# The last 2 KB a partition of wq moved from the sync queue to a GpSimd DMA whose source has eight outer rows

## The chip, the cores and the metric

The kernel runs on one core of one Trainium2 chip. The metric is device time in microseconds (us) of one execution; less is better. The profiled execution lists its engines as PE (TensorE matmul) and PEld (its weight load), DVE (VectorE), ACT (ScalarE), POOL (GpSimd) and SP (SyncE). Sixteen DMA engines move data between HBM and SBUF for this core.

## The reference

One decode step for two batch rows (B = 2, D = 512): a layer norm of x, a sliding-window attention over a cache, and a gated MLP that multiplies it.

```python
x = A_x                                  # (2, 1, 512)
xn = layernorm(x)
# attention: 32 query heads of 128, 8 kv heads, the last W = 4096 keys of 32768
q = (xn @ wq).reshape(B, 1, 32, 128)     # wq: 512 x 4096
s = softmax(q k^T * 128**-0.5) v         # k, v: (2, 8, 4096, 128) of the cache, each kv head for 4 query heads
s = s.reshape(B, 1, 4096) @ wo           # wo: 4096 x 512
# MLP: w_in 512 x 1792, Fh = 896, w_out 896 x 512
z = gelu(xn @ w_in); z1, z2 = z[:896], layernorm(z[896:])
g = silu((z1 * (z2 * w_sp + b_sp)) @ w_out)
return x + s * g
```

Everything is float32. The inputs that are read add up to the 89.4 MB that the DMA table of the profile lists: the k and v windows are 16 loads of 4 MB, wq 8 MB, wo 8 MB, w_in 3.5 MB, w_out 1.75 MB.

## The kernel before

**Loads.** Big loads go out on the sync (SP) queue in a fixed order: win, wout, wq, then k0, k1, v0, k2, v1, ... k7, v6, v7, then wo. They live in a ring of four slots of 32 KB a partition (`ring`, `bufs=4`): a load is issued when the tile that held its slot before has been read for the last time. `slot()` makes such a tile. wout uses the `kts` pool. The loop at lines 127 to 131 makes the two wq tiles: the one for k = 0, 1 is loaded by one DMA, the one for k = 2, 3 by two DMAs of 16 KB a partition each (2 MB each). With `wq_v = wq.rearrange("(p k) f -> p k f")`, partition p of plane k holds row 4p + k of wq. Four small loads (x, w_sp, b_sp and x again as x4) go out on the scalar (ACT) queue. GpSimd (POOL) issues no DMA; it clears constant tiles with memsets at the start (`nc.gpsimd.memset`) and builds the identity.

**Layer norm and transposed x.** On DVE `bn_stats`, `bn_aggr` and a few small steps give `xn` (2 x 512). Four PE transposes bring it into `pt` with partition p of plane k holding feature 4p + k, and a DVE copy puts it into `xnT` (128 x 4 x 32, the 30 other columns zero).

**First matmuls.** PE multiplies xnT with win (32 matmuls, `z`), turns z (28 matmuls, `zT_ps`), then the query projection: `queries(k)` issues eight matmuls for plane k, over r = 0, 1 and g = 0 to 3, with the 512 columns `c = (r * G + g) * 512` of `wqt[k]`, summed over k in two PSUM banks. `queries(3)` is the last. Then come y (hT with wout), two ACT copies `qs`, two DVE transposes `qx`, two DVE multiplies `xm`, one matmul `qa`, and `place_queries` (DVE, tile `qb`).

**Attention.** Eight units of two kv heads each run through steps whose order is written out by hand in `ORDER`: eight DVE transposes of the k tile into `kts`, score matmuls `sh`, softmax, DVE transposes `pT`, matmuls `acc` with v. Then wo: `part` for the blocks that can be multiplied early, and `so` for the last unit's rows. The second wo tile is loaded in pieces of 16, 8, 4, 2 and 2 KB a partition, and the last eight `so` matmuls take the last piece. The end is two DVE operations `res` and one store.

InOrder keeps PE, DVE, ACT and SP instructions in program order. POOL's order is left to the scheduler.

Of the kernel before, what the change touches and what calls it, by code (L numbers as in the profile page):

```python
# [9 lines left out]
F32 = mybir.dt.float32  # L10
# [4 lines left out]
P = 128  # L15
HQ, DH = 32, 128
# [4 lines left out]
def free_ap(t, offset, dims):  # L21

    return bass.AP(tensor=t.tensor, offset=t.offset + offset, ap=[list(t.ap[0])] + [list(d) for d in dims])
# [47 lines left out]
def kernel(  # L71
# [13 lines left out]
    nc = tc.nc  # L85
    pe, dve, act, sp = (InOrder(tc, e) for e in (nc.tensor, nc.vector, nc.scalar, nc.sync))
    B, _, D = x.shape
# [7 lines left out]
    KT = D // P  # L95
# [3 lines left out]
    DC = D // G  # L99
    SCALE = DH ** -0.5  # L100
    OFF = 30000.0 / SCALE

    fit = ctx.enter_context(tc.tile_pool(name="fit", bufs=1))
    fit.tile([P, 480], F32, tag="fit", name="fit")
# [2 lines left out]
    cst = ctx.enter_context(tc.tile_pool(name="cst", bufs=1))  # L107
# [3 lines left out]
    def slot(name, *shape):  # L111
        return ring.tile([P, *shape], F32, tag="slot", name=name)

    def bank(name, *shape):
        return ps.tile([P, *shape], F32, tag="kt", name=name, bufs=2)
# [9 lines left out]
    wq_v = wq.rearrange("(p k) f -> p k f", p=P)  # L125
    wqt = []
    for a in range(0, KT, 2):
        t = slot(f"wq{a}", 2, HQ * DH)
        for k, n in ((0, 2),) if a == 0 else ((0, 1), (1, 1)):
            sp.dma_start(t[:, k : k + n], wq_v[:, a + k : a + k + n, :])  # L130
        wqt += [t[:, 0], t[:, 1]]

    wb1 = cst.tile([1, 2], F32, tag="wb1", name="wb1")
# [21 lines left out]
    ident = cst.tile([P, P], F32, tag="ident", name="ident")  # L155
    make_identity(nc, ident)
    selw = cst.tile([P, 60], F32, tag="selw", name="selw")
    nc.gpsimd.memset(selw, 0.0)
    xnT = cst.tile([P, KT, 32], F32, tag="xnT", name="xnT")
    nc.gpsimd.memset(xnT, 0.0)  # L160
    ones = cst.tile([P, P], F32, tag="ones", name="ones")
    nc.gpsimd.memset(ones, 1.0)
# [29 lines left out]
    rsqrt(rs, va, "x")  # L192
    xn = sb.tile([B, D], F32, tag="o", name="xn", bufs=1)
    dve.tensor_scalar(xn, xs, mv[:, 0:1], rs, op0=ALU.subtract, op1=ALU.mult)
    pt = bank("xnT_ps", KT, B)
    for k in range(KT):
        pe.transpose(pt[:, k, :], xn.rearrange("b (p k) -> b k p", k=KT)[:, k, :], ident[:B, :B])
    dve.tensor_copy(xnT[:, :, :B], pt)

    same = cst.tile([P, G, 32], F32, tag="same", name="same")  # L200
# [15 lines left out]
    dve.tensor_reduce(other, free_ap(rowm, 0, [[4, 2], [8, REP]]), axis=AX.X, op=ALU.add)  # L216
    dve.tensor_scalar(other, other, -OFF, OFF, op0=ALU.mult, op1=ALU.add)
    diag = cst.tile([P, 4], F32, tag="diag", name="diag")
# [33 lines left out]
    pt = bank("zT_ps", 2, FT, B)  # L252
# [7 lines left out]
    pq = [ps.tile([P, 512], F32, tag=f"s{r}", name=f"q_ps{r}") for r in range(NR)]  # L260

    def queries(k):
        for r in range(NR):
            for g in range(G):
                c = (r * G + g) * 512
                pe.matmul(
                    pq[r][32 * g : 32 * g + 32, :], xnT[:, k, :], wqt[k][:, c : c + 512],
                    start=(k == 0), stop=(k == KT - 1),
                )

    queries(0)
    zT = cst.tile([P, 2, FT, B], F32, tag="zT", name="zT")
    dve.tensor_copy(zT, pt)
# [19 lines left out]
    per_b = [[0, FT], [1, B]]  # L293
    mean_over_rows(mean, z2, "mean_ps")
    queries(1)
    dve.tensor_scalar_mul(mean, mean, 1.0 / FH)
    dve.tensor_sub(z2, z2, free_ap(mean, 0, per_b))
# [5 lines left out]
    dve.tensor_scalar(z2, z2, wb[:, 0:1], wb[:, 1:2], op0=ALU.mult, op1=ALU.add)  # L303
    dve.tensor_mul(hT[:, :, 0 : 16 * B : 16], z1, z2)
    queries(2)
    queries(3)

# [286 lines left out]
    for u in range(NU):  # L594
        p = Unit()
        p.u, p.m, p.kt, p.sh, p.ss, p.s, p.p, p.pT = u, None, {}, {}, {}, {}, {}, {}
        units.append(p)
    for line in ORDER.strip().split("\n"):
        for name in line.split():
            name, at = name.split(":")  # L600
            u, _, a = at.partition(".")
# [34 lines left out]
```

## Time and profile before

| what | value |
|---|---|
| median of 3 runs | 216.96 us (216.91 to 217.72) |
| the profiled execution's own time | 217.3 us |
| its span, first to last instruction | 215.4 us |
| mean granted TensorE clock | 0.834 |
| busy: PE, DVE, ACT, POOL | 139.0, 125.7, 51.1, 5.2 us |
| HBM bytes read | 89.40 MB |

The span is 1.9 us shorter than the execution's own time, and that execution is 0.34 us above the median. In the profile, a group of instructions is listed as line, engine, operation, output tile <- input tiles, then counts and times; "L65" is the helper that issues every instruction of the in-order engines. A DMA group is listed where it is issued; "DMA k<-in_A_k_cache_dram" in the chain of work means that the time was spent until such a load had landed. The windows view gives, for each stretch, the busy time of each engine, the granted clock, the mean busy share of the 16 DMA engines, and GB/s.

### The profile page before, as it was taken

To read this page: it belongs to the slowest core of one execution; us is meant where nothing else is said; L and a number is where in the kernel's file an instruction comes from. 1 tells how busy PE (TensorE), PEld (TensorE's weight loads), DVE (VectorE), ACT (ScalarE), POOL (GpSimd) and SP (SyncE) were. 2 spreads that over 40 slices of the span, in tenths; PEclk is the share of its full clock that TensorE was granted. 3 is DMA by queue.
4 is the path that set the end of the run, shared out by engine and by line. 5 is a ranking of instruction groups with operands and counts; after the bars stand their busy time and mean duration, and the time that the engine had idled before them with its cause. 6 is when DMAs were issued, how large, how long until landed. Compare 5 with 4: busy or idle time off the path is not lost.

```text
span 215.4 us, 2476 instructions
## 1 busy us (share of the span) xinstructions
PE 139.0 (65%) x972; PEld 50.7 (24%) x972; DVE 125.7 (58%) x217; ACT 51.1 (24%) x128; POOL 5.2 (2%) x19
## 2 busy tenths in 40 slices
PE   0179594503857985934890796289359628988893
PEld 0118431300111222302230231113113211243242
DVE  2511212349799899639927981994698099535001
ACT  5010203200116036122330503151251306152210
POOL 8000000000000000000000000000000000000000
PEclk9999589955785799995899599559859985997999
DMA  7999999999999999999999999999999999999990
GB/s 256 427 438 456 396 435 456 408 458 408 463 414 441 426 426 444 417 458 408 450 420 444 423 420 450 426 450 417 438 415 444 432 420 456 405 463 402 414 377 29
DMA packets 3930, 89.54 MB, mean 416 GB/s; under 512 B 446, under 2 KB 462, under 8 KB 848
## 3 DMA queue, kind: packets, MB, share of 16 engines
q1 hardware_dynamic: 3900, 89.40, 96.8%
q8 instruction: 7, 0.11, 0.2%
q14 instruction: 3, 0.02, 0.0%
q10 hardware_dynamic: 20, 0.01, 0.0%
HBM read 89.40 MB, written 0.00 MB: 415 GB/s over the span
## 4 chain that ended last, share of the span: by engine, by line
DMA 68%; DVE 23%; ACT 3%; PE 2%; issue 1%; SPq 1%
DMA k<-in_A_k_cache_dram 51%; DVE kts L65 18%; DMA wo<-in_A_wo_dram 12%; DMA win<-in_B_w_in_dram 5%; DVE pT L65 2%; ACT p L65 2%; PE sh L65 2%; DVE m L65 1%; DVE gate L65 1%; SPq L65 1%; DVE nb L65 1%; PE s L65 1%; DVE qb L65 1%; ACT ss L65 0%; DVE res L65 0%
## 5 line engine op out<-in xcount | busy, mean ns | idle before, releaser
L65 DVE STREAM_TRANSPOSE kts<-k 128x1024 f32<-128x1024 f32 x64 | 75.6, 1218 | 31.2 <-DMA k<-in_A_k_cache_dram 31.2
L65 PE MATMUL sh<-kts,qb 128*32 128x512 f32 x256 | 43.4, 803 | 15.5 <-DVE kts L65 12.0
L65 PE MATMUL acc<-v,pT 128*32 128x512 f32 x256 | 35.1, 665 | 6.5 <-DMA v<-in_A_v_cache_dram 4.3
L65 ACT ACTIVATE p<-s,nb 128x512 f32<-128x512 f32 x32 | 22.5, 730 | 38.8 <-DVE nb L65 38.8
L65 ACT ACTIVATE ss<-sh 128x512 f32<-128x512 f32 x16 | 9.6, 598 | 62.0 <-PE sh L65 62.0
L65 PE MATMUL mo<-mg,joint 128*128 128x16 f32 x16 | 4.2, 342 | 26.0 <-DVE mg L65 26.0
L65 DVE STREAM_TRANSPOSE pT<-p 128x1024 f32<-128x1024 f32 x16 | 19.6, 1225 | 2.3 <-ACT p L65 2.1
L65 PE MATMUL s<-ss,sums 128*128 128x512 f32 x32 | 17.9, 642 | 2.5 <-ACT ss L65 2.5
L65 PEld LDWEIGHTS sh<-kts,qb 128*32 128x32 f32 x256 | 9.1, 129 | 37.3 <-issue 33.4
L65 PEld LDWEIGHTS acc<-v,pT 128*32 128x32 f32 x256 | 10.6, 142 | 30.9 <-issue 21.7
L65 DVE TENSOR_REDUCE m<-s 128x1 f32<-128x512 f32 x16 | 10.8, 673 | 4.8 <-PE s L65 4.8
L65 ACT ACTIVATE o<-acc,wd 128x128 f32<-128x128 f32 x32 | 9.1, 368 | 15.3 <-PE acc L65 15.3
L65 PE MATMUL q_ps<-wq,xnT 128*32 128x512 f32 x64 | 9.0, 689 | 5.2 <-DMA wq<-in_A_wq_dram 5.2
L65 PEld LDWEIGHTS mo<-mg,joint 128*128 128x128 f32 x16 | 3.4, 263 | 29.8 <-DVE mg L65 26.9
L65 PE MATMUL z<-win,xnT 128*32 128x448 f32 x32 | 4.9, 742 | 4.5 <-DMA win<-in_B_w_in_dram 4.5
L65 PEld LDWEIGHTS s<-ss,sums 128*128 128x128 f32 x32 | 4.9, 191 | 11.0 <-issue 8.2
L65 PE MATMUL part<-wo,oT 128*32 128x512 f32 x48 | 6.2, 595 | 1.0 <-DMA wo<-in_A_wo_dram 1.0
L65 PE MATMUL zT_ps<-rowm,z 128*128 128x2 f32 x28 | 6.6, 370 | 0.0
L65 PEld LDWEIGHTS zT_ps<-rowm,z 128*128 128x128 f32 x28 | 6.5, 325 | 0.0
L65 ACT ACTIVATION_READ_ACCUMULATOR p<-s,nb 128x1 f32 x32 | 6.3, 197 | 0.0
L65 ACT ACT_TABLE_LOAD x4 | 5.1, 1283 | 2.6 <-POOL hT L164 2.6
L65 DVE TENSOR_REDUCE o<-col 128x32 f32<-128x128 f32 x6 | 1.6, 270 | 6.9 <-PE col L65 6.9
(108 smaller groups left out, 70.3 us busy)
## 6 DMA issues: line engine op xcount, KB each, us to landing
k<-in_A_k_cache_dram SPq DMA_DIRECT2D x8, 4096.0 KB, 26.8
v<-in_A_v_cache_dram SPq DMA_DIRECT2D x8, 4096.0 KB, 31.7
wq<-in_A_wq_dram SPq DMA_DIRECT2D x1, 4096.0 KB, 24.4
wq<-in_A_wq_dram SPq DMA_DIRECT2D x2, 2048.0 KB
wo<-in_A_wo_dram SPq DMA_DIRECT2D x1, 4096.0 KB, 31.8
win<-in_B_w_in_dram SPq DMA_DIRECT2D x1, 3584.0 KB, 11.3
wo<-in_A_wo_dram SPq DMA_DIRECT2D x1, 2048.0 KB
wout<-in_B_w_out_dram SPq DMA_DIRECT2D x1, 1792.0 KB, 15.1
```

The source lines that it names most:

```text
L65: return self.tc.keep_in_program_order(call(*args, **kwargs))
```

## The change

The last 512 columns (2 KB a partition, 256 KB in all) of plane k = 3 of wq leave the second of the two 2 MB loads on the sync queue and are loaded by a DMA that GpSimd issues. Its source is written with three dimensions, 8 x 16 x 512: outer index c steps one partition row of wq (4 wq rows), the middle index d steps eight. Partition 16c + d of the tile so holds row 4(8d + c) + 3 of wq in these columns, another order of rows than the rest of the tile has. To match, a fifth plane of xnT holds the features of k = 3 in that order: a DVE copy `xnl` reorders xn, a fifth PE transpose brings it into `pt`, and the copy into xnT takes ten columns in place of eight. In `queries(3)` the matmul of the last 512 columns takes this plane. Ahead of that DMA GpSimd issues a load of 13 rows of 64 bytes of x into a tile `aside` that nothing reads.

```diff
+    LAST, FEW = 512, 8
...
-        for k, n in ((0, 2),) if a == 0 else ((0, 1), (1, 1)):
-            sp.dma_start(t[:, k : k + n], wq_v[:, a + k : a + k + n, :])
+        if a == 0:
+            sp.dma_start(t, wq_v[:, a : a + 2, :])
+        else:
+
+            of, to = wq_v[:, a : a + 2, :].rearrange("p k f -> p (k f)"), t.rearrange("p k f -> p (k f)")
+            n, at = 2 * HQ * DH - LAST, wq.offset + KT * HQ * DH - LAST
+            sp.dma_start(to[:, : HQ * DH], of[:, : HQ * DH])
+            sp.dma_start(to[:, HQ * DH : n], of[:, HQ * DH : n])
+            few = [[KT * HQ * DH, FEW], [FEW * KT * HQ * DH, P // FEW], [1, LAST]]
+            aside = cst.tile([13, 16], F32, tag="aside", name="aside")
+            nc.gpsimd.dma_start(aside, bass.AP(tensor=x.tensor, offset=x.offset, ap=[[16, 13], [1, 16]]))
+            nc.gpsimd.dma_start(to[:, n:], bass.AP(tensor=wq.tensor, offset=at, ap=few))
...
-    xnT = cst.tile([P, KT, 32], F32, tag="xnT", name="xnT")
+    xnT = cst.tile([P, KT + 1, 32], F32, tag="xnT", name="xnT")
...
-    pt = bank("xnT_ps", KT, B)
+    xnl = cst.tile([B, FEW, P // FEW], F32, tag="xnl", name="xnl")
+    dve.tensor_copy(xnl, xn.rearrange("b (d c k) -> b c d k", c=FEW, k=KT)[:, :, :, KT - 1])
+    pt = bank("xnT_ps", KT + 1, B)
...
+    pe.transpose(pt[:, KT, :], xnl.rearrange("b c d -> b (c d)"), ident[:B, :B])
...
+                rows = KT if k == KT - 1 and c >= HQ * DH - LAST else k
-                    pq[r][32 * g : 32 * g + 32, :], xnT[:, k, :], wqt[k][:, c : c + 512],
+                    pq[r][32 * g : 32 * g + 32, :], xnT[:, rows, :], wqt[k][:, c : c + 512],
```

In the built program the load of `aside` stands first on POOL, ahead of all memsets of the kernel, and the wq load stands last, behind the memsets of oT. On SP the number and order of loads stay as they were; the load of k2, which takes the slot of this wq tile, waits in addition for the GpSimd DMA.

## The prediction

> **What bounds the kernel now.** I read the DMA table first, then the end of the chain of waits, then the windows. Queue q1 is SP's, q10 ACT's; q8 and q14 fetch instructions.
>
> ```profile
> q1 hardware_dynamic: 3900, 89.40, 96.8%
> q8 instruction: 7, 0.11, 0.2%
> q14 instruction: 3, 0.02, 0.0%
> q10 hardware_dynamic: 20, 0.01, 0.0%
> ```
>
> SP's loads keep all 16 DMA engines busy for 96.8% of the span. The chain, in order of time, ends in such a load:
>
> ```profile
> 185.48 26.11 DMA wo<-in_A_wo_dram
> 211.59 0.04 issue
> 211.64 0.47 PE so L65 x8
> 212.11 0.02 issue
> 212.13 0.30 DVE res L65
> 212.43 0.02 issue
> 212.46 0.29 DVE res L65
> ```
>
> The last piece of wo is in at 211.59. What follows (eight matmuls, two DVE steps, the store, to 215.4) is 3.8 us and untouched. So the question is when the last DMA engine is done. The windows (columns: stretch, busy time of PE, PEld, DVE, ACT, POOL, clock, DMA share, GB/s):
>
> ```profile
> 36.00:184.00 148.00, 94.82 (x624) 29.87 (x624) 107.56 (x143) 37.59 (x99) 0.00 (x0) 0.79 1.00 433
> 208.00:209.00 1.00, 1.00 (x10) 0.14 (x2) 0.00 (x0) 0.00 (x0) 0.00 (x0) 1.00 0.98 391
> 209.00:210.00 1.00, 0.93 (x30) 0.74 (x32) 0.00 (x0) 0.60 (x1) 0.00 (x0) 1.00 0.68 264
> 210.00:211.00 1.00, 0.95 (x37) 0.68 (x28) 0.00 (x0) 0.00 (x0) 0.00 (x0) 1.00 0.35 135
> 211.00:212.00 1.00, 0.86 (x28) 0.39 (x19) 0.00 (x0) 0.00 (x0) 0.00 (x0) 1.00 0.02 6
> ```
>
> Two things. Between 36 and 184 no engine rests (1.00), and one moves 433 / 16 = 27.06 GB/s, or 16 KB in 0.605 us. And the engines do not stop together: the share falls from 0.98 to 0.02 over three microseconds. Stopping together, they would be done at 208 + 0.98 + 0.68 + 0.35 + 0.02 = 210.03, some 1.2 us before the last one (about 211.25). That 1.2 us bounds what any sharing out of bytes can bring.
>
> Who is late? The trace's records of single packets give start, length, size and queue. On each engine they follow one another without a gap, so I laid them end to end into 16 chains. Last wo byte of each chain, in us, F where an instruction fetch lies in it:
>
> ```
> 208.94 209.00 209.12a 209.29a 209.43 209.61aF 209.62 209.63
> 210.52F 210.56F 210.56F 210.70F 210.80F 210.81aFF 210.85F 211.25F
> ```
>
> Eight are early (to 209.63), eight late (from 210.52): the late ones carry q8's seven fetches of 16 KB, or (210.81) two of q14's three. "a" marks the four that carry ACT's load of x4, whose source has 4 outer rows. The q10 row bears that out: loads of 2, 1, 1 and 4 outer rows give 2 + 1 + 1 + 8 data packets and 2 + 1 + 1 + 4 completion words, the 20 listed, if a load of n outer rows goes to n engines. So 8 outer rows should mean 8 engines.
>
> **The change part by part.**
>
> *The bytes.* 256 KB leave q1: 16 KB fewer on every engine, -0.605 us each. They come back as 128 rows of 2 KB on eight engines: 16 rows, 32 KB each. At the full rate that is 1.21 us, net +0.605 on the eight, -0.605 on the others. A packet of another queue may cost more than its bytes. From above: q8's 0.2% of 16 engines' 215.4 us is 6.9 us, 0.98 us for a fetch of 16 KB that would take 0.605, so 0.38 too much; on each of 16 packets that would be 6 us, on the eight engines. From below: q10's share prints as 0.0%, under 1.7 us for its 20 packets, under 0.09 us each with two of 2 KB among them. q10 is the nearest row, a queue of small load packets beside q1, so I take 0.08 us a packet (2 KB at 27.06 GB/s is 0.076): 1.28 us, net **+0.68 us** on the eight. Nothing to gain below 1.21. One surcharge of 0.5 us in all (an engine turning to a strange queue once) stays in the range.
>
> *Where the eight lie* decides the sign, and the trace of before shows no GpSimd DMA:
> - only early engines: the last becomes 211.25 - 0.605 = 210.64, the early ones at most 209.63 + 0.68 = 210.31: **-0.61 us**;
> - some late one, but not the last: 210.81 + 0.68 = 211.49 (210.85 gives 211.53): **+0.24 us** (to +0.28);
> - the last one too: **+0.68 us**.
>
> A block of eight neighbours among 16 holds any given engine in 8 of 16 positions and avoids eight given late ones in at most one. The four "a" engines hold one late engine, 210.81, and not the last.
>
> [...]
>
> *The added instructions.* POOL's program begins with the 13-row load, ahead of the memsets; everything behind it on POOL moves by its issue. DVE's first step waits for POOL's identity, and the copy `xnl` and a fifth transpose come before xnT:
>
> ```profile
> 0.74 0.56 ACTq L65 DMA_DIRECT2D xs<-in_A_x_dram  x1
> 1.66 0.37 DVE L65 TENSOR_REDUCE rowm<-ident 128x32 f32<-128x128 f32 x1 [1.66 <-POOL ident masks.py:199]
> 4.71 1.04 POOL L365 MEMSET oT<- 128x512 f32 x3
> 6.34 0.53 DVE L65 TENSOR_SCALAR xn<-xs,mv,rs 2x512 f32<-2x512 f32 x1
> 7.02 0.61 PE L65 MATMUL xnT_ps<-ident,xn 2*128 2x2 f32 x4 [7.02 <-DVE xn L65]
> 7.66 0.17 DVE L65 COPY xnT<-xnT_ps 128x8 f32<-128x8 f32 x1 [0.79 <-PE xnT_ps L65]
> 12.16 4.86 PE L65 MATMUL z<-win,xnT 128*32 128x448 f32 x32 [4.54 <-DMA win<-in_B_w_in_dram]
> ```
>
> An issue took ACT 0.56 us; for POOL I take 1 us (bounds: 0 and, untested, several). xnl lies between the 0.17 and 0.53 of its neighbours, say 0.25; one transpose is 0.61 / 4 = 0.15. Together 1.4 us, hidden by the wait for win: xnT is done at 7.83, z starts at 12.16, 4.3 us of cover. Were POOL's issue over 3.9 us, z and all behind it would slip by the rest, and the next cover would take it (below).
>
> *The wq piece.* It is POOL's last instruction, behind the oT memsets that end at 5.75; with the 1 us ahead and its own issue it leaves near 8 us. If an engine alternates between queues packet by packet, 17 rounds of one SP packet (28 or 32 KB, 1.06 or 1.21 us) and 0.08 us take about 21 us: landed by 30. It is needed at the end of queries(3):
>
> ```profile
> 36.62 1.92 PE L65 MATMUL q_ps<-wq,xnT 128*32 128x512 f32 x16 [2.97 <-DMA wq<-in_A_wq_dram]
> 38.60 0.53 SPq L65 DMA_DIRECT2D k<-in_A_k_cache_dram  x1
> 42.33 1.14 PE L65 MATMUL qa<-xm,same 128*128 128x256 f32 x2 [2.26 <-DVE xm L65]
> 46.27 1.25 DVE L65 STREAM_TRANSPOSE kts<-k 128x1024 f32<-128x1024 f32 x1 [4.09 <-DMA k<-in_A_k_cache_dram]
> 47.44 1.18 DVE L65 TENSOR_TENSOR qb<-qa,grpm 128x1024 f32<-128x1024 f32 x1
> ```
>
> About 7 us to spare. If it is later, PE stands in queries(3) with y and qa queued behind it, DVE waits for qx, and SP waits to issue k2; but DVE stands idle for 4.09 us until k0 lands, and qb follows only at 47.44 while qa ends at 43.47: another 4 us of cover.
>
> *SP and the middle.* SP issues as many DMAs in the same order; k2 (38.60) waits for one more semaphore, which by the above has long come. Loads land up to 0.7 us earlier or later, and slots come free as much later. That starves nobody: a 4 MB load needs 4.19 / 433 = 9.7 us and lands, by the list of issues, 26.8 us after its issue, so 17 us of other loads are queued ahead.
>
> ```profile
> k<-in_A_k_cache_dram SPq DMA_DIRECT2D x8, 4096.0 KB, 26.8
> ```
>
> *Sum.* All compute edits are hidden; what is left is the last engine. I choose the middle case: 217.3 + 0.24 = 217.54 for an execution like the profiled one. That one is 0.34 above the median of the runs, so against the median: 216.96 + 0.24 = **217.2 us**.
>
> **The rivals.**
> 1. *Slower by the last engine:* the eight hold the engine that stops at 211.25: +0.68, or +1.2 with the surcharge: 217.6 to 218.2. It decides as soon as that one is among them. For: 8 of 16 positions. Against: none of the four "a" engines is the last.
> 2. *Faster:* the eight are the early ones: -0.61 (with the surcharge 209.63 + 1.18 = 210.81, -0.44): 216.35 to 216.5. For: early and late split just eight to eight, 0.9 us apart (209.63 to 210.52). Against: the "a" group holds both kinds, so the late ones are not a block that begins anywhere.
> 3. *Small packets of a foreign queue cost as the fetches do,* up to 6 us over: 217.2 + 0.9 and beyond, to 223. Against: the q10 row.
> 4. *It doesn't do what it says:* the DMA spreads over all 16 engines, 16 KB off and 16 KB on each: +0.07, 217.0, or the tail lands so late that queries(3) stalls beyond its cover. [...]
>
> **How the numbers follow.** Middle case 0.40, rival 1 0.20, rival 2 0.25, rival 3 0.10, rival 4 0.05. A measurement here can tell about 0.5%, 1.08 us. Rival 2 stays within it even at its best, so faster gets 0.05 for a better spread than I can see; slower gets rival 3 and the dear half of rival 1, 0.20; 0.75 remains for the same. The range goes from 216.3 (rival 2) to 218.2 (rival 1 with the surcharge) and leaves out rival 3.
>
> **What would show it.** A GpSimd queue in the DMA table with 128 packets and 0.26 MB; its share times the span over 128 is the price of a packet (0.08 us, about 0.3%). z still starting near 12.1, queries(3) near 36.6, k0 near 46.3. Then the last so matmuls: before 211.2 is rival 2, 211.7 to 212.0 the middle, 212.3 and later rival 1. A share of DMA of 0.35 or more in the last full microsecond means engines together, so rival 2. I am wrong if a stage before 200 us moves by over 1 us, for then a wait took the place of the bytes.

## The result, and the profile after

The changed kernel takes **219.01 us** (median of 4 runs, 218.97 to 219.49) against 216.98 us before: ratio **1.0088, 95% interval 1.0067 to 1.0110**. It is slower by 2.0 us. The forecast of 217.2 and its range to 218.2 were wrong. The span of the profiled execution went from 215.4 to 217.2 us.

The end first. The chain of waits of the changed kernel, in order of time:

```profile
187.66 25.72 DMA wo<-in_A_wo_dram
213.38 0.04 issue
213.42 0.47 PE so L65 x8
```

The last piece of wo lands at 213.38, 1.79 us later than before (211.59); what follows is unchanged. So the loss lies in the DMA engines again. Are they all later, or a few? The last microseconds in the windows view of the changed kernel (DMA share is the last number but one):

```profile
209.00:210.00 1.00, 1.00 (x16) 0.39 (x12) 0.00 (x0) 0.00 (x0) 0.00 (x0) 1.00 0.95 387
210.00:211.00 1.00, 1.00 (x11) 0.17 (x3) 0.00 (x0) 0.00 (x0) 0.00 (x0) 1.00 0.92 365
211.00:212.00 1.00, 1.00 (x34) 0.91 (x32) 0.00 (x0) 0.60 (x1) 0.00 (x0) 1.00 0.58 227
212.00:213.00 1.00, 1.00 (x38) 0.77 (x32) 0.00 (x0) 0.00 (x0) 0.00 (x0) 1.00 0.19 74
```

Stopping together, the engines would be done at 209 + 0.95 + 0.92 + 0.58 + 0.19 = 211.64, against 210.03 before. **1.6 us of the 1.8 is common to all engines**; only 0.2 us is a wider spread. The bytes that were moved add up to the same, so somewhere time was lost by all. The windows that find it, before:

```profile
8.00:10.80 2.80, 0.00 (x0) 0.00 (x0) 1.70 (x17) 0.00 (x0) 0.00 (x0) 1.00 0.90 389
10.80:18.00 7.20, 5.84 (x38) 2.16 (x38) 1.31 (x3) 1.09 (x2) 0.00 (x0) 1.00 1.06 455
18.00:36.00 18.00, 13.45 (x78) 7.79 (x78) 3.94 (x21) 3.20 (x5) 0.00 (x0) 0.81 1.00 427
```

and after:

```profile
8.00:10.80 2.80, 0.32 (x3) 0.24 (x3) 2.04 (x19) 0.00 (x0) 0.00 (x0) 1.00 1.00 430
10.80:18.00 7.20, 5.49 (x36) 1.84 (x36) 1.13 (x2) 1.09 (x2) 0.00 (x0) 1.00 1.03 342
18.00:36.00 18.00, 13.69 (x76) 8.43 (x79) 2.84 (x16) 2.07 (x4) 0.00 (x0) 0.72 1.00 428
36.00:184.00 148.00, 95.04 (x616) 29.52 (x608) 107.03 (x148) 38.58 (x101) 0.00 (x0) 0.80 1.01 433
```

From 10.8 to 18 us the engines are as busy as before (share 1.03 against 1.06) and move 342 GB/s in place of 455 (divided by the share, 332 in place of 429). The bytes not moved are (455 - 342) x 7.2 us = 0.81 MB, 1.9 us at 433 GB/s; the stretch ahead of it gives 0.3 us back (430 against 389). Behind 18 us no such difference shows (428 GB/s against 427, then 433 as before). And 10.8 us is when the new load begins to move. The DMA table of the changed kernel, and its issues:

```profile
q1 hardware_dynamic: 3900, 89.13, 96.4%
q0 software_dynamic: 176, 0.26, 0.4%
...
wq<-in_A_wq_dram POOLq DMA_DIRECT2D x1, 256.0 KB, 11.4
```

```profile
6.90 0.71 POOL L141 DMA_DIRECT2D wq<-in_A_wq_dram  x1
8.36 0.17 DVE L65 COPY xnT<-xnT_ps 128x10 f32<-128x10 f32 x1 [0.61 <-PE xnT_ps L65]
12.52 4.91 PE L65 MATMUL z<-win,xnT 128*32 128x448 f32 x32 [4.19 <-DMA win<-in_B_w_in_dram]
28.58 3.64 PE L65 MATMUL q_ps<-wq,xnT 128*32 128x512 f32 x16 [4.31 <-DMA wq<-in_A_wq_dram]
43.37 1.12 PE L65 MATMUL qa<-xm,same 128*128 128x256 f32 x2 [2.26 <-DVE xm L65]
48.70 1.25 DVE L65 STREAM_TRANSPOSE kts<-k 128x1024 f32<-128x1024 f32 x1 [5.47 <-DMA k<-in_A_k_cache_dram]
```

GpSimd's queue q0 carries 64 packets of 4 KB (two rows each), 64 of 8 bytes, 13 of 64 bytes (the 13-row load) and 35 of 4 bytes. The compute edits are hidden as foreseen: xnT at 8.53, z at 12.52, qa done at 44.5 while k0 comes at 48.70. Loads that were on their way at the time are late: wq's first tile by 2.5 us (28.58 against 26.05), k0 by 2.4 (48.70 against 46.27).

In the records of single packets, laid into 16 chains as in the prediction, eight engines carry the 4 KB packets, eight the 8-byte ones. Before, a packet of the sync queue takes the same time whenever its size is the same (28 KB 1.06 us, 32 KB 1.21, 16 KB 0.61), but for its first packets and behind an instruction fetch. I call what it takes beyond that its *stretch*. Between 5 and 30 us it sums over the engines to 0.0 us before and to 23.7 us after: about 1.1 to 1.3 us on each of the eight engines with the new data, and 1.6 to 1.8 us on **each** of the eight that got nothing but 8-byte packets. With the new packets' own extra (64 at 0.195 us on average, 12.5 us, against 9.7 at the full rate) that is (23.7 + 2.8) / 16 = 1.66 us an engine: the 1.6 us.

### The profile page after: what moved, and what is told of

It is laid out like the page before. It is cut to its first block, busy times and chain, and to the rows that moved or that the text cites. A ratio compares the mean times of both kernels' runs of the same rounds, so it can differ in the third digit from the quotient of the medians.

```text
span 217.2 us, 2482 instructions
## 1 busy us (share of the span) xinstructions
PE 140.7 (65%) x973; PEld 51.3 (24%) x973; DVE 125.9 (58%) x218; ACT 51.1 (24%) x128; POOL 6.5 (3%) x21
## 4 chain that ended last, share of the span: by engine, by line
DMA 68%; DVE 22%; PE 5%; ACT 3%; issue 1%; SPq 1%; ACTq 0%
DMA k<-in_A_k_cache_dram 51%; DVE kts L65 16%; DMA wo<-in_A_wo_dram 12%; DMA win<-in_B_w_in_dram 5%; PE sh L65 3%; DVE pT L65 2%; ACT p L65 2%; PE s L65 1%; DVE m L65 1%; DVE gate L65 1%; SPq L65 1%; DVE nb L65 1%; ACT ss L65 1%; DVE qb L65 1%; DVE res L65 0%
## 5 line engine op out<-in xcount | busy, mean ns | idle before, releaser
L65 PE MATMUL sh<-kts,qb 128*32 128x512 f32 x256 | 42.7, 792 | 17.4 <-DVE kts L65 13.3
L65 PE MATMUL s<-ss,sums 128*128 128x512 f32 x32 | 19.8, 703 | 2.3 <-ACT ss L65 2.3
L65 PEld LDWEIGHTS acc<-v,pT 128*32 128x32 f32 x256 | 10.8, 144 | 31.7 <-issue 22.5
L65 DVE TENSOR_REDUCE m<-s 128x1 f32<-128x512 f32 x16 | 10.8, 675 | 6.5 <-PE s L65 6.4
L65 PE MATMUL q_ps<-wq,xnT 128*32 128x512 f32 x64 | 9.5, 717 | 5.1 <-DMA wq<-in_A_wq_dram 5.1
L65 PEld LDWEIGHTS mo<-mg,joint 128*128 128x128 f32 x16 | 3.2, 249 | 26.4 <-DVE mg L65 23.7
L65 PE MATMUL xnT_ps<-ident,xn 2*128 2x2 f32 x4 | 0.6, 252 | 7.6 <-DVE xn L65 7.6
```

Source lines behind the costliest of these rows:

```text
L65: return self.tc.keep_in_program_order(call(*args, **kwargs))
```

## The experiments

The rival theories, in the order in which they came up. A: each packet of GpSimd's queue costs its engine a turn. B: only bytes count, and the eight lie on late engines. C1: the order in which the source is read holds up the memory. C2: the way in which the destination is spread over the engines does it; C2a: engines write partitions that other engines write in the sync queue's loads; C2b: the eight engines as such. D: the later start of POOL.

One view for all, from the packet records: the stretch between 5 and 30 us, summed over the 16 engines, beside the time and the ratio to the kernel before.

```
run               us      ratio (95%)              stretch, us   engines with data
before            216.98  -                         0.0          -
changed           219.01  1.0088 (1.0067 to 1.0110) 23.7         8
e1_aside_only     217.03  1.0005 (0.9993 to 1.0016)  0.0         (13 rows only)
e2_no_aside       219.02  1.0099 (1.0072 to 1.0125) 21.8         8
e3_pool_128rows   217.16  1.0008 (0.9990 to 1.0027)  0.2         16
e4_act_8outer     219.33  1.0102 (1.0079 to 1.0125) 24.2         8
e5_natural8       217.05  0.9997 (0.9976 to 1.0017)  0.6         16
e6_perm16         217.90  1.0037 (1.0023 to 1.0051) 10.5         16
e7_contig8        217.09  0.9995 (0.9980 to 1.0011)  0.1         16
f1_rows15         219.24  1.0104 (1.0076 to 1.0132) 26.3         8
f2_contig17       219.11  1.0093 (1.0072 to 1.0114) 23.9         8
f3_pitch512k      217.05  1.0011 (0.9995 to 1.0027)  0.3         16
f4_4kb            221.76  1.0215 (1.0186 to 1.0244) 56.1         8
g1_own            219.59  1.0125 (1.0110 to 1.0140) 10.0         8
g2_foreign        220.36  1.0169 (1.0151 to 1.0188)  9.1         8
g3_step4          217.27  1.0014 (1.0003 to 1.0024)  0.0         8
g4_neighbours     217.78  1.0032 (1.0015 to 1.0049)  8.2         8
```

**The 13-row load alone, and the change without it.**

```diff
# e1: the kernel before, and
+        if a:
+            aside = cst.tile([13, 16], F32, tag="aside", name="aside")
+            nc.gpsimd.dma_start(aside, bass.AP(tensor=x.tensor, offset=x.offset, ap=[[16, 13], [1, 16]]))
# e2: the changed kernel without these two lines
```

> The kernel before with only the 13-row load of x added on GpSimd; wq stays wholly on the sync queue. If the GpSimd queue costs every DMA engine about 0.2 us for each packet it brings (theory A, 8 packets an engine in the changed kernel), this load brings one row and one completion word: at most 0.3 us, 217.0 to 217.3. If the later start of POOL's memsets and of DVE behind them is the loss (theory D), it stays nearly whole: 218.5 or more.

> The changed kernel without the 13-row load; the 8-row wq load stays on GpSimd. Theory A (price per packet): the loss stays, 218.6 to 219.1, wherever the eight engines lie. [...]

e1 stands at the time before, so neither the 13 rows nor POOL's shift costs anything (217.03 us, 1.0005): D is out. e2 keeps the whole loss (219.02), as A says. In both e2 and the changed kernel the eight engines with data include all four that carry x4.

**Another shape on the same queue, the same shape on another queue.**

```diff
# e3: GpSimd, 128 outer rows, natural order
+            nc.gpsimd.dma_start(to[:, n:], of[:, n:])
# e4: e2 with the scalar queue
-            nc.gpsimd.dma_start(to[:, n:], bass.AP(tensor=wq.tensor, offset=at, ap=few))
+            act.dma_start(to[:, n:], bass.AP(tensor=wq.tensor, offset=at, ap=few))
```

> The same 256 KB on GpSimd, but with the 128 partitions as outer rows in their natural order, no 13-row load and no permuted plane of xnT: 16 engines with 16 KB each, so 4 packets of 4 KB an engine in place of 8. Theory A: about half the loss, 217.8 to 218.2. Theory B: no engine gets more bytes than before, 217.0. Theory C (the eight-row source order reads HBM badly and holds everybody up): 217.0.

> The 8-row wq load with the same source order, issued by the scalar queue in place of GpSimd, no 13-row load. Theory A as a property of GpSimd's queue: the loss goes, and what is left is the placing of the bytes, -0.4 to +0.7: 216.5 to 217.7. Theory C (source order) or a price of any second queue: 218.5 to 219.1. [...]

Windows of e3, then of e4:

```profile
10.80:18.00 7.20, 5.58 (x35) 1.75 (x35) 0.92 (x2) 1.09 (x2) 0.00 (x0) 1.00 1.01 430
```

```profile
10.80:18.00 7.20, 4.83 (x32) 1.21 (x32) 0.66 (x2) 1.09 (x2) 0.00 (x0) 1.00 1.02 361
```

Both misses for A: GpSimd's queue with four data packets an engine costs nothing, where half the loss was expected, and the loss stays with no GpSimd DMA at all. In e4 eight engines carry no packet of the load, yet their sync packets stretch by 1.6 to 1.8 us. The cause is neither a queue nor a packet's turn on its engine. That left the source's order and the destination.

**The source.**

```diff
# e5: 16 neighbouring rows a block   e7: one contiguous stretch
+            few = [[16 * KT * HQ * DH, 8], [KT * HQ * DH, 16], [1, 512]]    # e5
+            few = [[16 * 512, 8], [512, 16], [1, 512]]                      # e7
# e6: e2 with sixteen outer rows
-    LAST, FEW = 512, 8
+    LAST, FEW = 512, 16
```

> The 256 KB on GpSimd with 8 outer rows, but block c is 16 neighbouring partition rows of wq (64 KB apart) in place of every eighth row (512 KB apart); natural order, so no permuted plane, no 13-row load. Theory C1 (the 512 KB steps of the source hold up the memory for everybody): the loss goes, what is left is 16 KB more on eight engines, 217.2 to 217.7. Theory C2 (eight engines that write 16 neighbouring partitions each get in the way of the sync queue's writes): the loss stays, 218.6 to 219.2.

> The same 8 x 16 x 512 destination on GpSimd, but the source is one contiguous stretch of 256 KB at the start of wq (the last 512 columns of the query projection for k = 3 then use other weights, so that part of the result is left out). Theory C1: the loss goes, 217.2 to 217.7. Theory C2: it stays, 218.6 to 219.2.

> The changed kernel without the 13-row load and with 16 in place of 8 as the outer dimension (steps of 1 MB inside a block, partition 8c + d holds row c + 16 d): all 16 engines, 16 KB each. Theory C1: the loss stays or grows, 218.5 or more. Theory C2, read as a matter of too few engines: the loss goes, 217.0 to 217.3; read as a matter of engines that write neighbouring partitions: it stays in part, 217.8 to 219.

e5 and e7 looked like a victory for C1, but were not what they were meant to be: their two outer dimensions together are one even step over 128 rows, and the trace shows four packets of 4 KB on each of 16 engines, the case of e3, so the two ran as one. They say nothing on eight engines. e6, with 16 engines and blocks of eight neighbouring partitions, has 0.44 of the stretch and 0.9 us of loss. So the next three keep the dimensions apart (steps of 15 or 17 make no even step over 128 rows, and f1 and f2 ran on eight engines), or keep 128 rows and make the source bad.

```diff
+            few = [[15 * KT * HQ * DH, 8], [KT * HQ * DH, 16], [1, 512]]    # f1
+            few = [[17 * 512, 8], [512, 16], [1, 512]]                      # f2
+            few = [[8 * KT * HQ * DH, 128], [1, 512]]                       # f3, from the k cache
# f4: the changed kernel
-    LAST, FEW = 512, 8
+    LAST, FEW = 1024, 8
```

> GpSimd brings 256 KB with 8 outer rows to the same places as the changed kernel does, but block c is rows 15 c to 15 c + 15 of wq: steps of 64 KB within an engine's share and 960 KB between engines, in place of 512 KB and 64 KB. Some rows come twice and some not at all, so the last 512 columns of the query projection for k = 3 are left out in effect; no permuted plane, no 13-row load. The step of 15 keeps it at eight outer rows where the step of 16 ran as 128. Theory C1 (order in which the source is read): the stretch of the sync queue's packets goes, 217.0 to 217.7. Theory C2 (eight engines, each writing 16 neighbouring partitions): it stays, 218.6 to 219.2.

> As the run with steps of 15 rows, but each engine reads one contiguous stretch of 32 KB at the start of wq, 34 KB apart (again other weights in these columns). Theory C1: no stretch, 217.0 to 217.7. Theory C2: it stays, 218.6 to 219.2.

> The destination as in the run with 128 outer rows (16 engines, 217.2), but the 128 rows of 2 KB lie 512 KB apart in the k cache (so these columns hold other numbers). Theory C1, if it is the 512 KB step inside an engine's share that hurts: the stretch is back, 217.9 to 219. Theory C1, if it is the 64 KB between the rows that different engines read at a time, and theory C2: no stretch, 216.9 to 217.3.

> The changed kernel with LAST = 1024 in place of 512: 4 KB a partition, so twice the rows' length and 16 packets of 4 KB an engine on eight engines. If each packet of this transfer takes its time from all 16 engines: the loss doubles and the eight get 32 KB more each, 220.5 to 222. If it is a fixed price of the transfer: 219.0 to 219.7.

C1 is out: with a contiguous 32 KB an engine (f2) the loss is whole, with rows 512 KB apart in 128 rows (f3) it is gone. f4 has 56.1 us of stretch, 2.4 times, and 2.15% of loss: the price goes with the bytes and is not fixed.

**The destination.** One load of 64 KB on eight engines, to every fourth or to neighbouring partitions. g1 and g2 tried it first with eight small loads on the scalar queue (8 rows of 1920 bytes each, 123 KB in all, into a spare tile that nothing reads). C2a's forecasts for g1 to g4 rest on which engines write which partitions in the sync queue's loads. That was the author's assumption; the records name no partitions.

```diff
# g1, g2: behind the copy into xnT (pad is the tile of the pool "fit")
+    for i in range(8):
+        of = bass.AP(tensor=wq.tensor, offset=wq.offset + i * 8 * 512, ap=[[512, 8], [1, 480]])
+        act.dma_start(pad[4 * (i // 4) * 8 + i % 4 : 4 * (i // 4) * 8 + i % 4 + 29 : 4, :], of)    # g1
+        act.dma_start(pad[8 * i : 8 * i + 8, :], of)                                         # g2
# g3, g4: ahead of the memset of qb
+    of = bass.AP(tensor=wq.tensor, offset=wq.offset, ap=[[4 * 600, 8], [600, 4], [1, 512]])
+    nc.gpsimd.dma_start(qb[0:29:4, :2048].rearrange("p (c f) -> p c f", c=4), of)            # g3
+    nc.gpsimd.dma_start(qb[0:8, :2048].rearrange("p (c f) -> p c f", c=4), of)               # g4
```

> [...] Theory C2a (an engine that writes partitions which the sync queue's loads give to other engines gets in their way): no stretch of the sync queue's packets between 8 and 18 us, and the bytes alone, 15 KB more on eight engines: 217.0 to 217.6. Theory C2b (any second load on eight engines costs everybody): a stretch as in the run with neighbouring partitions.

> The same eight loads, bytes, engines and partitions in all, but load j goes to eight neighbouring partitions 8 j to 8 j + 7, one for each of eight engines. Theory C2a: the packets of the sync queue stretch by some 10 us summed over the 16 engines (the changed kernel: 23.5 us for 256 KB), and the time goes to 217.7 to 218.5. Theory C2b: the same as the run with steps of four partitions.

Neither is the test that it was meant to be: SP issued its three wq loads at 16.36 us (g1) and 16.73 us (g2) in place of 1.63, after a wait of 14.8 and 15.1 us for wout to land, and the DMA engines stood idle for a while. Windows of g1, then of g2:

```profile
10.80:18.00 7.20, 4.93 (x28) 1.29 (x32) 0.62 (x1) 0.54 (x1) 0.00 (x0) 1.00 0.90 343
```

```profile
10.80:18.00 7.20, 4.84 (x28) 1.22 (x32) 0.62 (x1) 0.54 (x1) 0.00 (x0) 1.00 0.80 315
```

A share of 0.90 and 0.80 says that the sync queue had run dry. The times hold this pause, and nearly all of the stretch lies in the first packets behind it: 9.8 of g1's 10.0 us, 8.4 of g2's 9.1. What can be read is the part ahead of the pause, where 24 of the 64 small packets (46 KB) were moved between sync packets. There, from 5 to 16 us, the sync packets take 0.0 us more than before in g1 and 0.4 us more in g2, where C2a let one expect some 10 us for the 123 KB, so near 4 for these 46. So one packet of 1920 bytes an engine to neighbouring partitions is not dear by itself.

> The kernel before plus one GpSimd load of 64 KB ahead of the memset of qb, into qb, which that memset then clears: 8 outer rows, each 4 pieces of 2 KB, to partitions 0, 4, 8, ... 28, so one engine writes each. [...] The two runs on the scalar queue shared semaphores with the sync queue's loads and held those up, so this one replaces them. Theory C2a (writing another engine's partitions is what hurts): the sync queue's packets stretch by under 1 us summed over the engines between 5 and 18 us, beside the first packets; 217.0 to 217.4. Theory C2b (eight engines are what hurts): 6 us, the changed kernel's 24 us for 256 KB scaled to 64 KB; 217.3 to 217.8.

> The same load to the neighbouring partitions 0 to 7. [...] Theory C2b: the same as with steps of four partitions.

Windows of g3, then of g4:

```profile
5.00:8.00 3.00, 0.61 (x4) 0.55 (x4) 1.47 (x9) 0.56 (x2) 0.00 (x0) 1.00 0.89 382
8.00:10.80 2.80, 0.00 (x0) 0.00 (x0) 1.69 (x17) 0.00 (x0) 0.76 (x1) 1.00 1.06 456
```

```profile
5.00:8.00 3.00, 0.61 (x4) 0.55 (x4) 1.45 (x9) 0.58 (x2) 0.00 (x0) 1.00 0.93 366
8.00:10.80 2.80, 0.00 (x0) 0.00 (x0) 1.71 (x17) 0.00 (x0) 0.00 (x0) 1.00 1.04 400
```

Eight engines carry the data in both, the four with x4 among them; same bytes, same queue; only the partitions differ. A window's GB/s rise and fall with its share, so they are compared divided by it. To every fourth partition: 429 and 430 GB/s, as before (389 / 0.90 = 432), every 4 KB packet takes 0.159 us, and the sync queue's packets keep their length (stretch 0.0). To neighbouring ones: 394 and 385 GB/s, the last packets take up to 0.24 us, and all 16 engines stretch, by 0.4 to 0.8 us each, 8.2 us in all. The times, 217.27 and 217.78, go the same way, but the intervals of their ratios overlap a little, so the stretch decides. The 8-byte packets are not the cause: e4 has none and keeps the loss, g3 has 16 and no stretch.

So it is the choice of partitions (stretch 0.0 us in g3, 8.2 in g4), and C2b falls. C2a gives one reason, that these partitions are written by other engines in the sync queue's loads, which no run shows. Another fits g3 and g4 as well: several engines that write the same few partitions at one time. g2's 0.4 us speaks against C2a as the whole reason, but no run separates the two. Nor does a run put the whole 256 KB on eight engines with g3's steps of four partitions; for the changed kernel the destination follows from g3 and g4 and from the sources and queues that e4, f2 and f3 rule out.

## Why the prediction was wrong, point by point

- **What bounds the kernel:** right. All of the loss is in the landing of wo, 1.79 us later, and no idle time of the DMA engines shows from 8 to 184 us (share 1.00 to 1.03).
- **The bytes:** this step failed. It priced the 256 KB at -16 KB on every engine and +0.68 us on eight, *net +0.605 on the eight, -0.605 on the others*, as if a packet cost only the engine that carries it. The runs showed a cost to all 16: 1.1 to 1.8 us of stretch on each, for which the sum had no term. With it, with the new packets' own time (12.5 / 8 = 1.56 us) and less the 0.605 us that left every engine, the packet records give some +2.2 us on the eight with data and +1.1 on the others. The distance between the two groups is near the forecast (1.1 against 1.28); what was missing is the part that all engines share. The eight without data, forecast to end earlier, ended later too: the first engine of all is done at 210.57 in the changed kernel, at 208.94 before.
- **The bounds of a packet's price** were taken from queues that add to an engine's own work. The q10 row could not show the cost: it holds 20 packets and two of 2 KB. The 0.08 us was about right for 2 KB in the runs without stretch (0.159 for 4 KB in e3 and g3). No run shows the 0.5 us surcharge in the upper end of the range; what the runs show in its place is the stretch on all 16.
- **Where the eight lie:** the middle case came out: the "a" engine with two of q14's fetches is among them and ends at 212.99, close to the last at 213.05 (which carries data too). But the spread between the engines grew by 0.2 us only; where the eight lie did not decide the sign. That the eight are a block of neighbours, and that the "a" engines would be among them, was the author's estimate, and the choice of the middle case rested on it. All four "a" engines are among the eight in the changed kernel, e2, g3 and g4; no record shows whether the eight are neighbours.
- **The compute edits, POOL's issue, the late piece, SP:** right. POOL's issues took 0.66 and 0.71 us, xnl 0.26; z, q and k0 kept their covers, and e1 shows no cost. The late piece came in eight packets of 4 KB an engine, not sixteen of 2 KB, and had landed 11.4 us after its issue, by 18.3 us and not by 30.
- **The signs:** its own sign of being wrong came, as wq's first tile and k0 landed over 2 us later. But no wait took the place of the bytes, as it had feared: the engines stayed busy and their packets took longer. The last so matmuls, at 213.42, lie where it put rival 1 (212.3 and later), and not for rival 1's reason.
- **Rivals:** rival 3 (foreign packets dear, 0.10) had the nearest time, with a mechanism that e3 refutes. Rival 4's +0.07 is a slip: 16 KB are eight rows at 0.08 us, 0.64 against 0.605, so +0.04; its 217.0 stands, and e3, which is this case, took 217.16. Rival 2 could hardly have worked for long: the engines with instruction fetches are not the same in every run. In the changed kernel the eight data engines carry the first two of q8's seven fetches, in g3 three of them.

## What to carry to other kernels

This load was not priced by its bytes and its engines alone: its partitions counted too. Beside the big loads, 256 KB with 128 outer rows (e3, 1.0008) and 64 KB to every fourth partition (g3, 1.0014) ran without stretch (0.2 and 0.0 us); 256 KB in eight blocks of 16 neighbouring partitions (the changed kernel, 1.0088) and 64 KB to 8 neighbouring ones (g4, 1.0032) did not (23.7 and 8.2 us). Whether another engine's partitions cost, or several engines on the same few, is open. When all DMA engines are busy and the GB/s of a window drop, as here (share 1.03, 342 GB/s in place of 455), look for packets that take longer, not for packets that are missing. And two outer dimensions that form one even step ran as one in e5 and e7 (four packets of 4 KB on each of 16 engines), so count packets before a run is taken as a test.

## What the runs showed of the hardware that was not expected

- In the changed kernel 256 KB on eight engines, in blocks of 16 neighbouring partitions, cost the 16 engines 1.5 us each on average, some 24 us of engine time, where their own transfer takes 9.7; blocks of half the length (e6, 16 engines, 8 neighbours a block) cost 10.5 us, twice the bytes (f4) 56.1.
- Whether GpSimd or the scalar queue (e4) issued the load made little difference: 23.7 and 24.2 us of stretch.
- GpSimd's load on eight engines came with eight 8-byte packets on each of the other eight (64 in the changed kernel), of about 0.01 us each; the one on 16 engines (e3) had none.
- Before, the seven instruction fetches of 16 KB took 0.88 to 0.96 us each and the packet behind each 0.47 to 0.55 us more than its size took elsewhere; seven of the eight engines that end late carry one each.
